# Pooled attention and SiLU MLP on one core: attention by token halves of the next tile instead of thirds of a batch, a ring of two tiles for x

## The chip, the core and the metric

The kernel runs on one core of a Trainium2 chip. TensorE (PE) does the matmuls, VectorE (DVE) and ScalarE (ACT) the elementwise work, GpSimd (POOL) pools keys and values in later tiles and issues most loads, SyncE (SP) issues the stores. The metric is the device time of one execution in microseconds (us), median of several runs. A span is the part of an execution that the profiler's instruction records cover.

## The reference

Eight batches of 576 tokens, eight heads of width 64. Keys and values are first averaged over groups of 8 positions, so that each head has 72 pooled keys. The attention output, 4608 tokens by 512 channels, is the input x of a two-layer network with 2048 hidden channels:

```python
k_p = k.reshape(B, H, Sp, pool, D).mean(axis=3)      # pool = 8, Sp = 72
v_p = v.reshape(B, H, Sp, pool, D).mean(axis=3)
scores = scale * np.matmul(q, k_p.transpose(0, 1, 3, 2))
scores = scores - np.max(scores, axis=-1, keepdims=True)
attn = np.exp(scores)
attn = attn / (np.sum(attn, axis=-1, keepdims=True) + 1e-09)
x = np.matmul(attn, v_p)      # heads side by side: 4608 x 512
h = x @ w_in                  # 512 x 2048
g = h * (1.0 / (1.0 + np.exp(-h)))
return g @ w_out              # 2048 x 512
```

## The kernel before

**Tiles and batches.** The network works on nine tiles of 512 tokens (`t` = 0 to 8), attention on eight batches of 576. The two don't line up: batch b ends 64 (b+1) tokens further on than tile b. While the matrix products of tile t run, the attention of batch t+1 is worked in between them; the last two tiles have none beside them. x (`xT`) lies in SBUF as a ring of 2304 columns (`NX = 4 * S`, four batches, 4.5 tiles).

**The matrix products.** Most of a tile is done by a Strassen-like scheme with seven products in place of eight 2x2 block products. In the first product there are four units of hidden channels (a, b, c, d), each with products 1 to 7 of two steps; in the second, products P1/Q1 to P7/Q7 (two halves of four steps). A step is two matmuls of 256 columns (one of 512 in the plain products `g`, `m`). `tile_products` walks an order written out by hand, such as `FOUR` (tiles 2 to 6) or `BARE` (7 and 8); `FIRST` and `THREE` are tiles 0 and 1, where weights and sums are still being loaded and made. Sums of blocks are made by DVE: `unit_x_sum` for x, `hidden_sum` for the hidden values, `weight_sum` and `unit_weight_sum` for weights. Each group of products goes through three PSUM banks A, E and B; `behind` copies A to B after product 1 (DVE), copies E to SBUF after product 5 (ACT, L738) and after product 6 adds B and that copy into E (DVE, L740). Product 7 then goes on adding into B, so it has to wait until L740 has read it.

**Attention work** is a list of fillers, `at(step, function)` or `late(step, function)`: `spread` runs each when the product's step has been issued. All engines get their instructions in program order; nothing is reordered. `third(n)` is a third of a batch: 192 positions of each of the two groups of four heads, 384 columns. `scores` does 16 matmuls of 192 columns into four banks (L414), then four exponentials on ACT (L425); `denominators` 4 matmuls of 384 columns (L435), then a logarithm and an exponential on ACT (L444, L445), which give the reciprocal; `numerators` 16 matmuls (L464) and two multiplications on DVE that write x (L476). In a middle tile they stand at steps 63 (scores of third 0), 77 (scores 1 and denominators 0), 87 (denominators 1, numerators 0 and the numerators of the batch before's third 2), 94 (scores 2), 103 (denominators 2) and 106, or 103 again (numerators). Tile 6 does its own third 2 as well. Batch 0 is done ahead of tile 0 in halves of 256 positions (`scores0` and so on), and its last 64 positions ride along in tile 0 (`rest`).

**PSUM** has eight banks: a pool of three (`mm`) for the products' B banks and the second product, one of five (`at`) for attention and the units' A and E.

**ACT tables.** The exponentials and logarithms need another function table than SiLU. `attn_tables` (L483) and `moe_tables` (L486) load one, 1.28 us each; the latter stands ahead of every tile.

**Loads.** Up to tile 1 everything comes through POOL's queue, in the order of the program: the rest of batch 0's queries, keys of batch 1, `w_out` quarter 0, all queries of batch 1, `w_out` 1 to 3, values of batch 1, then, as fillers, the keys of batch 2 in two halves, the second of which is added onto the first by the transfer itself (`load_half_2`), with the queries of batch 2 between them, and the values of batch 2 in the same way. Each load waits for the landing of the one eight before it in the program (they share eight semaphores in turn). The second halves' sums over the pooled positions are made by DVE in `slot_sums` (L260), for batch 2 at step 2 of tile 1.

Of the kernel before, what the change touches and what calls it, by code (L numbers as in the profile page):

```python
# [36 lines left out]
def kernel(  # L37
# [21 lines left out]
    HS = S // 2  # L59

    KQ, NQ, CQ = KG // 2, NTT // 2, d_model // 2

    NX = 4 * S
# [4 lines left out]
    QF = QI // 2  # L68
    DH = D // 2
    VW = max(HS, 2 * S // 3)  # L70
# [44 lines left out]
    xT = singles.tile([128, KF, NX], BF16, name="xT")  # L115
# [17 lines left out]
    def load_q(b, halves=False):  # L133
        st = batches.setdefault(b, {})
        q_bf = mid.tile([128, 2, QI * D], BF16, tag="q_bf", name="q_bf")
        if halves:
            pass
        elif b == B - 1:

            for s in range(4):  # L140
                for a in range(2):
                    nc.gpsimd.dma_start(
                        out=q_bf[QP * s : QP * (s + 1), a, :].rearrange(
                            "p (i d) -> p i d", d=D
                        ),
                        in_=q[b, 4 * a + s].rearrange("(i p) d -> p i d", p=QP),
                    )
        else:
            nc.gpsimd.dma_start(out=q_bf, in_=q_r[b])
        st["q_bf"] = q_bf  # L150
        st["qT"] = mid.tile([128, 2, QI, QP, 2], BF16, tag="qT", bufs=1, name="qT")


    def q_transpose(b, a, f):
        q_positions(b, a, f * QF, (f + 1) * QF, batches[b]["qT"][:, a, f * QF : (f + 1) * QF])

    def q_positions(b, a, i0, i1, dst):
        nc.vector.transpose(
            out=dst.rearrange("r i p c -> r (i p c)").bitcast(FP32),
            in_=batches[b]["q_bf"][:, a, i0 * D : i1 * D].bitcast(FP32),  # L160
        )
# [143 lines left out]
    def copy_v(b, a, copy=nc.vector.tensor_copy, heads=4):  # L305
# [5 lines left out]


    IP = NQ // QP
    QR = QI - 2 * IP
    flat = [x.rearrange("p a b -> p (a b)") for x in h_sum]
    es_wide = flat[0][:SP].rearrange("k (s n) -> k s n", s=4)
    rec0 = flat[1].bitcast(FP32).rearrange("r (f g n) -> r f g n", f=2, g=2)
    wide32 = flat[2].bitcast(FP32)
    lnd_wide, rec_wide = wide32[:, :512], wide32[:, 512:]
    qT_rest = flat[3][:, : 2 * QR * 2 * QP].rearrange(  # L320
        "r (a i p c) -> r a i p c", a=2, i=QR, p=QP
    )

    def q_transpose0(a, f):
        cols = slice(f * IP, (f + 1) * IP)
        q_positions(0, a, f * IP, (f + 1) * IP, batches[0]["qT"][:, a, cols])

    def q_transpose_rest(a):
        q_positions(0, a, 2 * IP, QI, qT_rest[:, a])

    def scores0(pool, g, f):
        st = batches[0]
        sc = [pool.tile([128, 2, 512], FP32, tag="sc2", bufs=2, name="sc_ps") for _ in range(2)]
        for c in range(2):
            for s in range(4):
                rows = slice(32 * s, 32 * (s + 1))
                nc.tensor.matmul(
                    sc[s // 2][:SP, s % 2, :NQ],
                    lhsT=kz[0][rows, g, c, :],
                    rhs=st["qT"][rows, g, f * IP : (f + 1) * IP, :, c],  # L340
                    start=(c == 0), stop=(c == 1),
                )
        es = mid.tile([SP, 4, VW], BF16, tag="es", bufs=4, name="es")[:, :, :NQ]
        for j in range(2):
            nc.scalar.activation(
                es[:, 2 * j : 2 * j + 2, :], sc[j][:SP, :, :NQ], func=AF.Exp,
                scale=score_scale,
            )
        st["es", g, f] = es

    def denominators0(den_ps, f):
        for g in range(2):
            for s in range(4):
                nc.tensor.matmul(
                    den_ps[32 * s : 32 * (s + 1), g * NQ : (g + 1) * NQ],
                    lhsT=ones, rhs=batches[0]["es", g, f][:, s, :], start=True, stop=True,
                )
        nc.scalar.activation(lnd_wide, den_ps, func=AF.Ln)

    def reciprocals0(f):  # L360
        nc.scalar.activation(
            rec0[:, f].rearrange("r g n -> r (g n)"), lnd_wide, func=AF.Exp, scale=-1.0
        )

    def numerators0(nu_ps, g, f):
        st = batches[0]
        es = st.pop(("es", g, f))
        nu = nu_ps.rearrange("r (c n) -> r c n", c=2)
        for c in range(2):
            for s in range(4):  # L370
                nc.tensor.matmul(
                    nu[32 * s : 32 * (s + 1), c, :],
                    lhsT=st["vp"][:, 4 * g + s, c::2], rhs=es[:, s, :],
                    start=True, stop=True,
                )
        return nu

    def x_of(nu, g, f):
        nc.vector.tensor_mul(
            out=xT[:, 2 * g : 2 * g + 2, f * NQ : (f + 1) * NQ], in0=nu,  # L380
            in1=rec0[:, f, g : g + 1, :].broadcast_to([128, 2, NQ]),
        )

    QV = QI // 3

    def third(n):
        return tuple((g, n * QV, (n + 1) * QV) for g in range(2))

    def width(segs):
        return QP * sum(i1 - i0 for _, i0, i1 in segs)  # L390

    def seg_cols(segs):
        o = 0
        for g, i0, i1 in segs:
            n = QP * (i1 - i0)
            yield g, i0, i1, slice(o, o + n)
            o += n

    def rest_cols(segs, g):
        o, n = width(segs), QR * QP  # L400
        return slice(o + g * n, o + (g + 1) * n)

    def scores(b, segs, rest=False):
        st = batches[b]
        w = width(segs) + 2 * QR * QP * rest
        sc = [ps_tile([128, 512], FP32, "at", "sc_ps")[:SP, :w] for s in range(4)]
        jobs = [(g, b, st["qT"][:, g, i0:i1], cs) for g, i0, i1, cs in seg_cols(segs)]
        if rest:
            jobs += [(g, 0, qT_rest[:, g], rest_cols(segs, g)) for g in range(2)]
        for g, bk, qT, cs in jobs:  # L410
            for c in range(2):
                for s in range(4):
                    rows = slice(32 * s, 32 * (s + 1))
                    nc.tensor.matmul(  # L414
                        sc[s][:, cs],
                        lhsT=kz[bk % 2][rows, g, c, :],
                        rhs=qT[rows, :, :, c],
                        start=(c == 0), stop=(c == 1),
                    )
        if rest:  # L420
            es = es_wide
        else:
            es = mid.tile([SP, 4, VW], BF16, tag="es", bufs=4, name="es")[:, :, :w]
        for s in range(4):
            nc.scalar.activation(es[:, s, :], sc[s], func=AF.Exp, scale=score_scale)  # L425
        st["es", segs] = es


    def denominators(b, segs):
        st = batches[b]  # L430
        es = st["es", segs]
        w = es.shape[-1]
        den_ps = ps_tile([128, 512], FP32, "at", "den_ps")
        for s in range(4):
            nc.tensor.matmul(  # L435
                den_ps[32 * s : 32 * (s + 1), :w],
                lhsT=ones, rhs=es[:, s, :], start=True, stop=True,
            )
        if w > VW:
            lnd, rec = lnd_wide, rec_wide  # L440
        else:
            rec = mid.tile([128, VW], FP32, tag="rec", bufs=4, name="rec")[:, :w]
            lnd = mid.tile([128, VW], FP32, tag="lnd", name="lnd")[:, :w]
        nc.scalar.activation(lnd, den_ps[:, :w], func=AF.Ln)  # L444
        nc.scalar.activation(rec, lnd, func=AF.Exp, scale=-1.0)  # L445
        st["rec", segs] = rec

    def numerators(b, segs, rest=False):
        st = batches[b]
        w = width(segs)  # L450
        g0, i0, i1 = segs[0]
        c0 = b * S % NX + i0 * QP
        cols = slice(c0, c0 + (i1 - i0) * QP)
        es = st.pop(("es", segs))
        rec = st.pop(("rec", segs))
        jobs = [(g, st["vp"], cs) for g, _, _, cs in seg_cols(segs)]
        if rest:
            jobs += [(g, batches[0]["vp"], rest_cols(segs, g)) for g in range(2)]
        nu = []
        for c in range(2):  # L460
            nu_ps = ps_tile([128, 512], FP32, "at", "nu_ps")
            for g, vp, cs in jobs:
                for s in range(4):
                    nc.tensor.matmul(  # L464
                        nu_ps[32 * s : 32 * (s + 1), cs],
                        lhsT=vp[:, 4 * g + s, c::2],
                        rhs=es[:, s, cs],
                        start=True, stop=True,
                    )
            nu.append(nu_ps)  # L470
        ng = len(segs)
        done = [(c, slice(0, w), cols) for c in range(2)]
        if rest:
            done += [(c, slice(w, w + 2 * QR * QP), slice(2 * NQ, S)) for c in range(2)]
        for c, ws, xs in done:
            nc.vector.tensor_mul(  # L476
                out=xT[:, 2 * g0 + c : 2 * (g0 + ng - 1) + c + 1 : 2, xs],
# [630 lines left out]
```

## Time and profile before

| | us |
|---|---|
| median of 3 runs | 278.34 (278.17 to 278.71) |
| the profiled execution | 278.52 |
| its span | 276.7 |
| granted TensorE clock | 1.0 of full speed throughout |
| DVE, ACT busy | 208.5, 191.6 |

Where the tiles lie in the span, by the first matmul of each (timeline of PE):

| tile | from | to | length | attention worked in it |
|---|---|---|---|---|
| 0 | 17.8 | 51.48 | | batch 1 and 64 positions of batch 0 |
| 1 | 51.48 | 81.12 | 29.64 | batch 2 |
| 2 to 5 | 81.12 | 194.70 | 28.36, 28.43, 28.42, 28.37 | batches 3 to 6 |
| 6 | 194.70 | 223.61 | 28.91 | batch 7 |
| 7 | 223.61 | 248.21 | 24.60 | none |
| 8 | 248.21 | 276.7 | 28.5 with the last stores | none |

A page of the profile has, for each group of equal instructions, the busy time, the mean duration of one, and the idle time of its engine just ahead of them with the engine that ended it. A timeline row is: start, length, engine, line, operation, output and inputs, shapes, count, and in brackets idle time of that engine ahead of it and what ended it. Matmuls overlap: the time that one takes away is read from start to start (0.109 us for 256 columns, 0.218 for 512), not from its length.

### The profile page before, as it was taken

The numbers are of one execution on the slowest core, as the hardware profiler recorded it, in microseconds if no ns is written. First come the engines' busy times: TensorE is split into PE (matmuls) and PEld (weight loads), VectorE is DVE, ScalarE is ACT, GpSimd is POOL, SyncE is SP. The second block draws the span as 40 slices with busy tenths as digits, with TensorE's granted clock in tenths as the row PEclk, the third lists the DMA queues.
The fourth block names the chain that finished last, engine by engine and source line by source line (L and its number), as shares of the span: only waits on it lengthen the run. The fifth ranks groups of instructions, "written<-read, shape, count | busy, mean of one in ns | idle before, by whom it ended". The sixth has DMA issues, their size and how long they took to land.

```text
span 276.7 us, 7362 instructions
## 1 busy us (share of the span) xinstructions
PE 269.3 (97%) x3000; PEld 212.5 (77%) x3000; DVE 208.5 (75%) x381; ACT 191.6 (69%) x365; POOL 98.4 (36%) x104
## 2 busy tenths in 40 slices
PE   8999899999999999999999999999999999999994
PEld 4368544488788878887888778877887788888883
DVE  4868857987998777877787787768787786766872
ACT  1578758578769785979498958985798578409710
POOL 8657314262138620962088219850900000000000
PEclk9999999999999999999999999999999999999999
DMA  7999999967738797559655965999410042005004
GB/s 214 270 204 288 208 292 222 238 123 165 142 73 158 218 161 133 142 152 170 102 140 152 167 107 121 219 109 139 124 31 2 1 105 51 0 12 130 16 0 152
DMA packets 31761, 37.72 MB, mean 136 GB/s; under 512 B 10640, under 2 KB 22672, under 8 KB 31728
## 3 DMA queue, kind: packets, MB, share of 16 engines
q0 software_dynamic: 24080, 26.64, 52.3%
q1 hardware_dynamic: 7216, 9.97, 13.0%
q10 hardware_dynamic: 432, 0.66, 0.6%
q8 instruction: 23, 0.38, 0.6%
q14 instruction: 10, 0.08, 0.2%
HBM read 36.70 MB, written 9.44 MB: 167 GB/s over the span
## 4 chain that ended last, share of the span: by engine, by line
PE 87%; DVE 4%; issue 1%; ACT 1%; DVEq 0%
PE o_psB L725 16%; PE u_psB L706 15%; PE o_psA L725 10%; PE u_psE L706 10%; PE o_psE L725 10%; PE u_psA L706 10%; PE o_ps L623 4%; PE sc_ps L414 4%; PE nu_ps L464 2%; PE den_ps L435 2%; PE hp_ps L564 1%; DVE w_sum L538 1%; DVE xT L476 1%; ACT h_T L744 1%; DVE u_psE L740 1%
## 5 line engine op out<-in xcount | busy, mean ns | idle before, releaser
L706 PEld LDWEIGHTS <-w_sum 128*128 128x128 bf16 x528 | 51.3, 98 | 7.2 <-issue 1.2
L725 PEld LDWEIGHTS <-h_sum 128*128 128x128 bf16 x512 | 48.4, 98 | 8.8 <-issue 1.2
L706 PEld LDWEIGHTS <-w_in_sb 128*128 128x128 bf16 x396 | 38.7, 98 | 4.9
L725 PEld LDWEIGHTS <-h_T 128*128 128x128 bf16 x384 | 36.6, 98 | 6.1 <-issue 1.1
L706 PE MATMUL u_psB<-x_sum,w_sum 128*128 128x256 bf16 x264 | 39.1, 272 | 0.8 <-DVE u_psE L740 0.8
L706 PE MATMUL u_psA<-xT,w_in_sb 128*128 128x256 bf16 x264 | 39.8, 273 | 0.0
L425 ACT ACTIVATE es<-sc_ps 72x384 bf16<-72x384 f32 x80 | 32.2, 481 | 9.7 <-PE sc_ps L414 9.7
L725 PE MATMUL o_psB<-w_sum,h_sum 128*128 128x256 bf16 x256 | 32.7, 273 | 0.3 <-DVE o_psE L740 0.3
L725 PE MATMUL o_psA<-w_out_sb,h_T 128*128 128x256 bf16 x256 | 31.9, 272 | 0.0
L740 DVE TENSOR_TENSOR u_psE<-u_psB,p 128x512 f32<-128x512 f32 x33 | 22.4, 696 | 10.2 <-ACT p L738 8.6
L735 DVE COPY u_psB<-u_psA 128x512 f32<-128x512 f32 x31 | 21.4, 698 | 9.8 <-PE u_psA L706 9.8
L744 ACT ACTIVATE h_T<-u_psE 128x512 bf16<-128x512 f32 x33 | 19.7, 597 | 12.4 <-PE u_psE L706 12.4
L757 DVE TENSOR_TENSOR c<-u_psB,p 128x512 f32<-128x512 f32 x33 | 22.5, 682 | 4.3 <-PE u_psB L706 3.5
L188 POOL TENSOR_TENSOR raw<-raw 72x1024 f32<-72x1024 f32 x10 | 23.6, 2361 | 0.0
L744 ACT ACTIVATE h_T<-u_psB 128x512 bf16<-128x512 f32 x33 | 19.8, 600 | 4.4 <-PE u_psB L706 4.4
L649 DVE TENSOR_TENSOR h_sum<-h_T 128x1024 bf16<-128x1024 bf16 (+1 forms) x31 | 21.3, 699 | 1.1 <-ACT h_T L744 1.1
L744 ACT ACTIVATE h_T<-u_psA 128x512 bf16<-128x512 f32 x33 | 20.1, 608 | 1.5 <-PE u_psA L706 1.3
L744 ACT ACTIVATE h_T<-c 128x512 bf16<-128x512 f32 x33 | 21.0, 637 | 0.0
L649 DVE TENSOR_TENSOR h_sum<-h_T,h_sum 128x1024 bf16<-128x1024 bf16 (+1 forms) x24 | 20.4, 855 | 0.1
L706 PE MATMUL u_psE<-x_sum,w_sum 128*128 128x256 bf16 x132 | 19.8, 273 | 0.0
L706 PE MATMUL u_psE<-x_sum,w_in_sb 128*128 128x256 bf16 x132 | 19.8, 273 | 0.0
L476 DVE TENSOR_TENSOR xT<-nu_ps,rec 128x384 bf16<-128x384 f32 x40 | 19.7, 548 | 0.0
(108 smaller groups left out, 452.4 us busy)
## 6 DMA issues: line engine op xcount, KB each, us to landing
out_dram<-o_sb SPq DMA_DIRECT2D x128, 64.0 KB, 1.7
raw<-in_k_dram POOLq DMA_DIRECT2D x10, 576.0 KB, 8.5
raw<-in_v_dram POOLq DMA_DIRECT2D x10, 576.0 KB, 8.2
q_bf<-in_q_dram POOLq DMA_DIRECT2D x6, 576.0 KB, 9.7
w_in_sb<-in_moe_w_in_dram POOLq DMA_DIRECT2D x8, 256.0 KB, 8.0
w_out_sb<-in_moe_w_out_dram POOLq DMA_DIRECT2D x4, 512.0 KB, 12.2
raw<-in_v_dram POOLq DMA_DIRECT2D x2, 768.0 KB, 11.8
raw<-in_k_dram POOLq DMA_DIRECT2D x1, 768.0 KB, 8.8
```

What stands on the lines that cost most here:

```text
L188: nc.gpsimd.tensor_add(out=raw[:, :, : 2 * D], in0=raw[:, :, : 2 * D], in1=raw[:, :, 2 * D :])
L414: nc.tensor.matmul(sc[s][:, cs], lhsT=kz[bk % 2][rows, g, c, :], rhs=qT[rows, :, :, c], start=(c == 0), stop=(c == 1),)
L425: nc.scalar.activation(es[:, s, :], sc[s], func=AF.Exp, scale=score_scale)
L476: nc.vector.tensor_mul(out=xT[:, 2 * g0 + c : 2 * (g0 + ng - 1) + c + 1 : 2, xs], in0=nu[c][:, ws].rearrange("r (g n) -> r g n", g=ng), in ...
L623: nc.tensor.matmul(ps["m", m], lhsT=h_T[:, g, m * 128 : (m + 1) * 128], rhs=w_out_sb[:, g, :], start=(g == 0), stop=(g == KG - 1),)
L649: nc.vector.tensor_tensor(out=h_sum[n][:, k0:k1, :], in0=get(a), in1=get(b), op=op)
L706: nc.tensor.matmul(ps[y, BANK[n]][:, u, :], lhsT=w[:, kk, 128 * u : 128 * (u + 1)], rhs=x[:, kk, :], start=n in (1, 5) and u == 0 and kk == 0,
L725: nc.tensor.matmul(o_bank(n, c), lhsT=left(n, kt, c), rhs=w[:, kt, :], start=n in (1, 5) and kt == 0 and c == 0, stop=kt == KQ - 1, skip_g ...
L735: (acopy if t == 0 else vcopy)(ps[y, "B"], ps[y, "A"])
L740: tt(out=ps[y, "E"], in0=ps[y, "B"], in1=f32[y], op=add)
L744: nc.scalar.activation(h_T[:, g : g + 2, j * NQ : (j + 1) * NQ], src, func=AF.Silu)
L757: tt(out=c22, in0=ps[y, "B"], in1=f32[y], op=add)
```

## The change

Attention is cut by the tiles of the network. In tile t, for t = 0 to 7, the 512 positions of tile t+1 are worked as two halves of 256. A half that lies over the end of a batch takes two sets of matmuls (`half_units`), one for each batch, into the same banks. Scores, denominators and products of a half fill their banks (512 columns). x is a ring of two tiles; the transposed queries (`qT`) hold one tile. The fillers stand at three places of a middle tile: 63 (scores of half 0), 79 (scores of half 1, denominators of half 0) and 93 (denominators of half 1, all numerators); x is written by `x_half` at 93 and 97, the x sums stand at 105 in every tile, and the SiLU table is loaded at 94. Tile 7 uses `FOUR` and has the attention of tile 8 beside it.

In `FOUR` and `THREE` the second half of product 2 moves from two places to between Q6 and P7. In `FIRST`, two steps of the plain product m0 move ahead of d7, the others ahead of d4, and m3 (now in an `at` bank) goes ahead of the last quarter of the others. The queries of batch 1 are loaded in two pieces of 14 and 4 positions (of 18), for two head groups each: four transfers in place of one. The values of batch 1 go ahead of `w_out` 3, and the second piece behind it. The queries of later batches are loaded at step 33.

```diff
-    NX = 4 * S
+    UH = NQ // QP
+    UT = NTT // QP
...
-    xT = singles.tile([128, KF, NX], BF16, name="xT")
+    xT = singles.tile([128, KF, 2 * NTT], BF16, name="xT")
+    qT = singles.tile([128, 2, UT, QP, 2], BF16, name="qT")
...
+    def half_units(t, f):
+        for b, i0, i1, u in q_units(t, UH * f, UH * (f + 1)):
+            o = QP * (u - UH * f)
+            yield b, slice(u, u + i1 - i0), slice(o, o + QP * (i1 - i0))
+
+    def scores(t, f):
+        sc = [ps_tile([128, 512], FP32, "at", "sc_ps")[:SP] for s in range(4)]
+        for g in range(2):
+            score_matmuls(sc, t, f, g, g * NQ)
+        es = half_state(t, f)["es"] = es_tile()
         for s in range(4):
             nc.scalar.activation(es[:, s, :], sc[s], func=AF.Exp, scale=score_scale)
...
+    def x_half(t, f):
+        st = half_state(t, f)
         for c in range(2):
             nc.vector.tensor_mul(
+                out=xT[:, c::2, x_cols(t, f)],
+                in0=st["nu"][c].rearrange("r (g n) -> r g n", g=2),
+                in1=st["rec"].rearrange("r (g n) -> r g n", g=2),
             )
...
-    load_q(1)
-    for c in range(1, 4):
+    load_q(1, halves=True)
+    load_q_part(1, 0, 2 * UT - QI)
+    for c in range(1, 3):
         load_w_out(c)
     for i0, i1 in ((0, 3), (3, 4), (4, 5)):
         load_slots(nc.gpsimd, 1, "v", i0, i1)
+    load_w_out(3)
+    load_q_part(1, 2 * UT - QI, QI)
...
-    HEAD = "P1 ds Q1 d4 P2 o2:4-5 P5 Q5 P6 Q6 o2:5-8 P7 Q7 P3 Q3 P4 Q4"
+    HEAD = "P1 ds Q1 d4 P2 P5 Q5 P6 Q6 Q2 P7 Q7 P3 Q3 P4 Q4"
...
     FIRST = (
-        "p4.0 p6.0 p0.1 p2.1 c1 p4.1 c5 p6.1 c6 c2 c7 d1 c3 d5 c4 d6 cs d2 d7 m0:0-4 d3 ds d4"
-        " m1:0-4 m2:0-4 m0:4-8 m1:4-8 m2:4-8 m0:8-12 m1:8-12 m2:8-12"
-        " m0:12-16 m1:12-16 m2:12-16 m3:0-16"
+        "p4.0 p6.0 p0.1 p2.1 c1 p4.1 c5 p6.1 c6 c2 c7 d1 c3 d5 c4 d6 cs d2 m0:0-2 d7 d3 m0:2-4 ds d4"
+        " m1:0-4 m2:0-4 m0:4-8 m1:4-8 m2:4-8 m0:8-12 m1:8-12 m2:8-12 m3:0-12"
+        " m0:12-16 m1:12-16 m2:12-16 m3:12-16"
     )
...
             late(63, attn_tables)
-            for n, (sc, den) in enumerate(zip((63, 77, 94), (77, 87, 103))):
-                late(den, denominators, a, visits[n])
-                late(sc, scores, a, visits[n])
-            nu_at = (87, 103, 106)
-            for n, sg in enumerate(visits):
-                if n < 2 or t >= B - 2:
-                    late(nu_at[n], numerators, a, sg)
-                if n == 0 and 1 < t < B - 1:
-                    late(nu_at[n], numerators, a - 1, visits[2])
+            late(63, scores, a, 0)
+            late(79, scores, a, 1)
+            late(79, denominators, a, 0)
+            late(79, reciprocals, a, 0)
+            late(93, denominators, a, 1)
+            late(93, reciprocals, a, 1)
+            for n in range(2):
+                late(93, numerators, a, n)
+            late(93, x_half, a, 0)
+            late(94, moe_tables)
+            late(97, x_half, a, 1)
         if t < NT - 1:
             for n in (0, 2, 1, 3):
-                late(105 if t < 4 else 96 if t < B - 1 else 84, unit_x_sum, t + 1, n)
-        moe_tables()
+                late(105, unit_x_sum, t + 1, n)
```

## The prediction

> **What bounds the kernel now.** I read the busy shares first, then the stages.
>
> ```profile
> PE 269.3 (97%) x3000; PEld 212.5 (77%) x3000; DVE 208.5 (75%) x381; ACT 191.6 (69%) x365; POOL 98.4 (36%) x104
> ...
> 109.50:137.90 28.40, 28.40 (x338) 23.84 (x336) 21.80 (x39) 22.23 (x43) 12.75 (x10) 1.00 0.71 141
> ...
> 223.60:248.20 24.60, 24.60 (x226) 21.81 (x225) 18.01 (x29) 13.05 (x23) 0.00 (x0) 1.00 0.17 41
> ```
>
> The lower rows are busy times by stage (length, PE, weight loads, DVE, ACT, POOL, clock, DMA share, GB/s) of tile 3 and tile 7. PE is busy throughout and its list of waits sums to only some 3 us, so the time is what PE has to issue. A tile's 112 steps take 112 x 0.2186 = 24.48 us; tile 7, without attention, takes 24.60. Attention costs tile 3 some 3.9 us. The timeline of PE in tile 2 shows on what:
>
> ```profile
> 94.78 0.60 PE L706 MATMUL u_psB<-xT,w_sum 128*128 128x256 bf16 x4
> 95.31 0.54 PE L414 MATMUL sc_ps<-qT,kz 32*72 32x192 bf16 x16
> 95.80 1.25 PE L725 MATMUL o_psA<-w_out_sb,h_T 128*128 128x256 bf16 x10
> ...
> 98.64 0.38 PE L725 MATMUL o_psB<-w_sum,h_sum 128*128 128x256 bf16 x2
> 98.95 0.37 PE L435 MATMUL den_ps<-es,ones 72*32 72x384 bf16 x4
> 99.25 0.54 PE L414 MATMUL sc_ps<-qT,kz 32*72 32x192 bf16 x16
> 99.72 1.70 PE L725 MATMUL o_psB<-w_sum,h_sum 128*128 128x256 bf16 x14
> 101.26 0.82 PE L725 MATMUL o_psA<-w_out_sb,h_T 128*128 128x256 bf16 x6
> 102.01 0.35 PE L435 MATMUL den_ps<-es,ones 72*32 72x384 bf16 x4
> 102.18 0.83 PE L464 MATMUL nu_ps<-es,vp 72*32 72x192 bf16 x32
> 102.95 1.70 PE L725 MATMUL o_psB<-w_sum,h_sum 128*128 128x256 bf16 x14
> ```
>
> Take the products' starts, at 0.109 us a matmul, out of each gap. The first interruption costs 95.80 - (94.78 + 0.44) = 0.58; denominators and scores 99.72 - 98.86 = 0.86; denominators and two numerators 102.95 - 101.91 = 1.04. Two more in the tile cost 0.57 and 0.70. Sum 3.75; with the keys' transpose 0.13 and 24.48 this is 28.36, tile 2's length. Four matmuls run side by side: sixteen of 192 columns stream for 4 x 192 x 0.000427 = 0.33 us (0.000427 us a column from 0.109 per 256), so of the first 0.58 some 0.25 is change-over, before (0.09) and after.
>
> **Attention in halves, tiles 2 to 7.** The columns in all stay the same; the interruptions fall from five to three. Widening 192 to 256 adds 4 x 64 x 0.000427 = 0.11 to each sixteen, and 384 to 512 adds 0.05 to denominators. So: scores 0.69; scores and denominators 0.86 + 0.11 + 0.05 = 1.02; denominators and four sets of sixteen (two before) 1.04 + 0.05 + 2 x 0.11 = 1.31. Sum 3.02 against 3.75. A half over a batch's end splits its matmuls: in tile 0 now, 192 and 64 columns together take 0.60 where 256 would take 0.47 + 0.11, so 0.03 for each kind, 0.06 for a tile (1, 2, 4, 5 and 6).
>
> The new order puts back a wait. After product 6, L740 must read B before product 7 goes on:
>
> ```profile
> 28.46 0.60 PE L706 MATMUL u_psB<-x_sum,w_sum 128*128 128x256 bf16 x4
> 28.90 0.60 PE L706 MATMUL u_psA<-xT,w_in_sb 128*128 128x256 bf16 x4
> 29.92 0.60 PE L706 MATMUL u_psB<-x_sum,w_sum 128*128 128x256 bf16 x4 [0.42 <-DVE u_psE L740]
> ```
>
> Issue of product 6 ends at 28.90, product 7 starts at 29.92: 1.02. (c6 and c7 at 24.82 and 26.28, and product 6 and 7 of tile 1 at 73.57 and 74.59, give 1.02 too.) Between Q6 and P7 stand now six matmuls, denominators and numerators; afterwards only Q2's eight, 0.87. PE waits 0.15 in each of tiles 1 to 7. Bounds: 0, if L740 is quicker, and 0.4, as at 29.92; the three equal rows decide.
>
> A middle tile is then 24.48 + 0.13 + 3.02 + 0.15 and 0.05 on the mean = 27.83. Tiles 2 to 5: 113.58 now, 4 x 27.83 = 111.3 after, -2.3. Tile 6 (28.91 now, with its own third 2 at 0.54): -1.1. Tile 7 gets attention, without a keys' transpose: 24.48 + 3.02 + 0.15 = 27.65, +3.05. Together -0.3: what the cuts save, the eighth attended tile and the new wait take back.
>
> **What lies beside PE there.** Sixty-four exponentials of 512 columns in place of 80 of 384 and four of 512 (0.59 and 0.48 us), and a table pair of 2 x 1.28 more in tile 7: ACT has 13.05 of 24.60 us there, so they are hidden. x of the next tile is now finished in the last microseconds. Count from the end of Q6 = T. Product 7 starts at T+1.02; denominators and numerators go in after step 93, at T+2.33 to 3.63; Q3 ends at T+5.82, the tile at T+7.57. DVE: first x half T+3.2 to 4.4 (multiplication 0.6 from start to start, as L740), the sum behind Q7 to 5.0, second x half to 6.2 (its reciprocal is ready at T+5: 0.5 and 0.6 on ACT after T+3), E's copy from 6.1 to 6.8, four x sums (108.88 to 110.55 now, 1.67) to 8.45, then unit a's copy to 9.15. Next tile: a5 needs the first sum, ready at 7.2, at 8.04; a6 needs the copy at 9.35, 0.2 later than it is there. Nothing waits, but 0.2 is all the cover; each 0.1 beyond it costs 0.1 in seven tiles.
>
> **Tile 0.** Products m0:0-2 fill the wait at 29.92 (gain 0.44), and the wait of 0.39 to 0.55 ahead of the first m2 matmul (33.51) goes, since ACT gets d3 0.85 earlier: together 1.0. `w_out` 0 has landed at 29.45 (issued 20.95, 8.5 to landing), 0.1 after m0:0-2 wants it. The first scores then come at 35.0 but wait for the transposed queries: DVE starts these at 34.28 as now, two of 448 columns at some 0.6 (0.47 for 288, 0.43 for 256, a nanosecond a column), done at 35.45; 0.45 of the gain goes. Interruptions: now 0.69, 0.89, 0.84, 0.37, 0.66, 0.55, 0.54 = 4.54; after 0.69, 1.02, 0.37, 1.10 = 3.18. So tile 0 would end near 49.3 instead of 51.48.
>
> But tile 1 can't use it:
>
> ```profile
> 54.84 0.42 DVE L260 TENSOR_TENSOR raw<-raw 128x256 f32<-128x256 f32 x1 [0.37 <-DMA raw<-in_k_dram]
> 55.29 0.29 DVE L260 TENSOR_TENSOR k<-raw 128x128 bf16<-128x128 f32 x1
> 55.88 0.70 DVE L735 COPY u_psB<-u_psA 128x512 f32<-128x512 f32 x1 [0.30 <-PE u_psA L706]
> ```
>
> DVE sits at 54.84 until the last piece of batch 2's keys has landed, and the copy that b6 needs is next in its queue; after the change nothing in that queue moves in between. DMA share is 0.9 to 1.2 from 15 to 55, so what counts is the bytes ahead, and these are the same: values and `w_out` 3 change places, two small query pieces go behind them. The three extra transfers push those that wait for the eighth before them: the first halves of batch 2's keys go out at about 34.5, 37 and 39.4 (landings of `w_out` 1 at 34.8, `w_out` 2 at 37.3, values 42.3 less their move forward) instead of 31.8, 33.2 and 35.1, still ahead of the 44 at which the transfers before them end. So I leave 54.84. The copy runs 55.55 to 56.25, b6 starts at 56.3 (56.92 now), where PE would have come at 54.8 to 55.5. Of 2.2 gained, 0.6 is left. Bounds: 0, if the keys come 0.6 later, and 2.1, if they come before 53.3. `w_out` 3 itself moves from a landing at 39.9 to about 43.3; m0:12 wants it at 44.1.
>
> The Trainium skill speaks against the split of the query load: DMA: Bandwidth & Descriptors, Measured (HBM→SBUF, 128 partitions, SWDGE, issued from GpSimd), advises to batch towards 1 MiB, and Anatomy of one DMA there puts some 2.0 us of fixed cost on each. If the three extra ones paid that one after another, the keys would come 6 us later by the page's figure and the whole would end near 283 by this estimate. No row before shows such a serial cost.
>
> The row for it: landings of `w_out` 0, the queries (576 KB) and `w_out` 1, at 29.45, 32.2 and 34.8, while issue to landing is 8.5 to 11.3; transfers in the full queue cost their bytes, not their latency. I take nothing for the split, and up to 1 us (half of the spread from 8.5 to 10.7 of queries and `w_out` 0) for the range.
>
> **Tile 1 after b6.** Now 3.74 of attention (0.59, 0.86, 1.02 with 0.31 of waiting for L740, 0.57, 0.70); after 3.08 + 0.15: -0.5. **Tile 8** is unchanged, a wait of 0.03 apart.
>
> **Sum:** -0.6 (to b6), -0.5 (rest of tile 1), -0.3 (tiles 2 to 7), -0.03 = -1.45. The profiled execution is 278.52 (span 276.7 and 1.82 around it), 0.18 above the median; 278.52 - 1.45 = 277.1, or 276.9 beside the median 278.34.
>
> **Rivals.** First, the gain of tile 0 comes through: the second halves of the keys are issued when the first land (45.35 now), and the store of m0 at 43.6 is out of their way afterwards. Against it, the DMA share near 1 up to 55. Then -1.45 - 1.5 = -2.95: 275.4.
>
> Second, on the other side: the chain of DVE at the tile's end is late. Place: a6 of tiles 2 to 8; price: seven times what the chain exceeds its 0.2 of cover. For it: DVE has 9.15 - 3.2 = 6 us with hardly a gap, and a6 already starts 0.06 late in tile 3 (110.79 to 111.29, 0.50 instead of 0.44). Against it: that chain today has two multiplications more behind the copy of E. Slower than before from 0.2 + 1.45/7 = 0.41 late; at 0.6, +2.8 - 1.45 = +1.35: 279.7.
>
> Third, the change-overs are not saved, since they go with the kinds of matmuls rather than with the places: then tiles 1 to 6 gain half of 0.73 and tile 7 costs 0.35 more, so +2.2 + 0.35 goes onto -1.45: +1.1, 279.4. Against it: the denominators at 102.01 go straight on to the numerators in 0.17, their streaming time.
>
> Fourth, no difference: the waits at L740 are 0.3, so -1.45 + 7 x 0.15 = -0.4: 277.9.
>
> **How the numbers follow.** Forecast 0.48, first rival 0.20, second 0.12, third 0.06, fourth 0.14. What a measurement can tell from no change is about 0.2%, 0.56 us. Faster: 0.48 + 0.20, and 0.02 for a fourth rival at half its price = 0.70; within 0.2%: 0.13; slower: 0.17. Range: down to the first rival, 275.3; up, with 1 us for the keys and 0.4 of the waits, to 278.4. The forecast's own range, without rivals, is 276.2 to 277.8.
>
> **What will show it.** Middle tiles of 27.7 to 27.9 us and tile 7 of 27.6; three interruptions of 0.7, 1.0 and 1.3; a wait of 0.15 ahead of each P7, ended by DVE L670 (the old L740); in tile 1 a wait of 0.8 to 1.5 ahead of b6, ended by DVE, which waited for keys near 54.8. Wrong it is if the tiles' first steps show waits for x or its sums, if the keys land before 53.5 or after 56, or if m0's last quarter waits for `w_out`.

## The result, and the profile after

| | before | after |
|---|---|---|
| median, us | 278.34 (278.06 to 279.54, 13 runs) | 276.17 (275.44 to 277.67, 13 runs) |
| profiled execution, span, us | 278.52, 276.7 | 276.11, 274.3 |

The ratio is 0.9925, with an interval of 0.9907 to 0.9942: faster by 2.2 us. Forecast were 276.9, in a range of 275.3 to 278.4. The direction and the middle tiles came as written; two terms did not, by -1.76 and +0.96 us, and they pulled in opposite directions. So it is partly luck that the total came within 0.7 of the forecast.

The time by stages, first matmul to first matmul, from the timeline of PE:

| stage | before | forecast of the difference | after | difference |
|---|---|---|---|---|
| to b6 of tile 1 | 56.92 | -0.6 | 54.56 | -2.36 |
| the rest of tile 1 | 24.20 | -0.5 | 23.78 | -0.42 |
| tile 2 | 28.36 | -0.5 | 28.82 | +0.46 |
| tiles 3 to 5 | 85.22 | -1.7 | 83.27 | -1.95 |
| tile 6 | 28.91 | -1.1 | 27.77 | -1.14 |
| tile 7 | 24.60 | +3.05 | 27.62 | +3.02 |
| tile 8 | 28.49 | 0 | 28.49 | 0 |

The busy line of the page after, and the same windows as before the change (length, PE, weight loads, DVE, ACT, POOL, clock, DMA share, GB/s) for tile 3 and tile 7:

```profile
PE 267.4 (97%) x2967; PEld 213.6 (78%) x2972; DVE 209.6 (76%) x368; ACT 191.3 (70%) x337; POOL 99.9 (36%) x107
```

```profile
107.16:134.90 27.74, 27.74 (x303) 23.48 (x300) 21.43 (x37) 21.06 (x37) 12.66 (x10) 1.00 0.83 165
218.19:245.81 27.62, 27.62 (x299) 23.35 (x297) 21.30 (x35) 20.83 (x36) 0.00 (x0) 1.00 0.16 39
```

PE is still busy from end to end. Tile 7 now looks like tile 3: it has attention, and nearly the same length. The timeline of PE in tile 3 shows the three places:

```profile
120.83 0.60 PE L636 MATMUL u_psB<-xT,w_sum 128*128 128x256 bf16 x4
121.36 0.65 PE L331 MATMUL sc_ps<-qT,kz 32*72 32x256 bf16 x16
121.94 1.05 PE L655 MATMUL o_psA<-w_out_sb,h_T 128*128 128x256 bf16 x8
...
124.57 1.04 PE L655 MATMUL o_psB<-w_sum,h_sum 128*128 128x256 bf16 x8
125.53 0.65 PE L331 MATMUL sc_ps<-qT,kz 32*72 32x256 bf16 x16
126.11 0.40 PE L363 MATMUL den_ps<-es,ones 72*32 72x512 bf16 x4
126.45 1.05 PE L655 MATMUL o_psB<-w_sum,h_sum 128*128 128x256 bf16 x8
127.33 1.04 PE L655 MATMUL o_psA<-w_out_sb,h_T 128*128 128x256 bf16 x8
128.35 1.47 PE L655 MATMUL o_psB<-w_sum,h_sum 128*128 128x256 bf16 x12
129.75 0.40 PE L363 MATMUL den_ps<-es,ones 72*32 72x512 bf16 x4
129.98 1.05 PE L378 MATMUL nu_ps<-es,vp 72*32 72x256 bf16 x32
130.96 0.61 PE L655 MATMUL o_psB<-w_sum,h_sum 128*128 128x256 bf16 x4
```

Take out the products at 0.1092 us each, as before: 121.94 - (120.83 + 0.44) = 0.67; 126.45 - (124.57 + 0.87) = 1.01; 130.96 - (128.35 + 1.31) = 1.30. The sum is 2.98. Between Q2 at 127.33 and P7 at 128.35 lie 1.02 us, 0.15 more than Q2's eight matmuls take: the wait that the new order was to bring.

What was not foreseen stands at two places. The first is the keys of batch 2, in the timeline of DVE around the start of tile 1:

```profile
52.72 0.42 DVE L261 TENSOR_TENSOR raw<-raw 128x256 f32<-128x256 f32 x1 [0.36 <-DMA raw<-in_k_dram]
```

This is the row that stood at 54.84 before: the last piece landed 2.1 us earlier. Tile 1 began at 49.36, and b6 followed at 54.56, right behind c5: it waited for nothing.

The second is tile 2. The timelines of POOL, DVE and PE there:

```profile
88.50 2.36 POOL L189 TENSOR_TENSOR raw<-raw 72x1024 f32<-72x1024 f32 x1 [2.21 <-DMA raw<-in_v_dram]
90.94 1.59 POOL L192 TENSOR_TENSOR vp<-raw 72x512 bf16<-72x512 f32 x1
```

```profile
88.77 0.68 DVE L687 TENSOR_TENSOR c<-u_psB,p 128x512 f32<-128x512 f32 x1
89.37 2.03 DVE L579 TENSOR_TENSOR h_sum<-h_T 128x1024 bf16<-128x1024 bf16 x1
```

```profile
92.45 0.60 PE L636 MATMUL u_psB<-xT,w_sum 128*128 128x256 bf16 x4 [0.29 <-DVE c L687]
92.98 0.84 PE L331 MATMUL sc_ps<-qT,kz 32*72 32x192 bf16 x32
94.15 1.03 PE L655 MATMUL o_psA<-w_out_sb,h_T 128*128 128x256 bf16 x8 [0.33 <-DVE o_psB L665]
```

POOL waited 2.21 us for the values of batch 3. Its pooling then ran while DVE was to make a hidden sum, and that sum took 2.03 us where the others take 0.68. The DVE instructions behind it came late, and PE waited for two of them. Before the change the pooling was over at 91.53, and the first hidden sum began at 92.15 (POOL and DVE of the kernel before):

```profile
87.80 2.38 POOL L188 TENSOR_TENSOR raw<-raw 72x1024 f32<-72x1024 f32 x1
90.26 1.27 POOL L191 TENSOR_TENSOR vp<-raw 72x512 bf16<-72x512 f32 x1
```

```profile
92.15 0.68 DVE L649 TENSOR_TENSOR h_sum<-h_T 128x1024 bf16<-128x1024 bf16 x1
```

Tile 2 now begins 2.8 us earlier, but the values come 1.1 us later: their second half landed at 88.42, before the change at 87.34. The first half was asked for 3.5 us earlier (68.26 for 71.75) and took 10.8 us to land, where it had taken 6.8.

### The profile page after: what moved, and what is told of

Same layout as the page of the kernel before. It is cut to its first block, busy times and chain, and to the rows that moved or that the text cites. A ratio compares the mean times of both kernels' runs of the same rounds, so it can differ in the third digit from the quotient of the medians.

```text
span 274.3 us, 7266 instructions
## 1 busy us (share of the span) xinstructions
PE 267.4 (97%) x2967; PEld 213.6 (78%) x2972; DVE 209.6 (76%) x368; ACT 191.3 (70%) x337; POOL 99.9 (36%) x107
## 4 chain that ended last, share of the span: by engine, by line
PE 86%; DVE 5%; issue 1%; ACT 0%; DVEq 0%; ACTq 0%
PE o_psB L655 16%; PE u_psB L636 15%; PE o_psE L655 10%; PE u_psE L636 10%; PE o_psA L655 10%; PE u_psA L636 10%; PE o_ps L553 5%; PE sc_ps L331 3%; PE nu_ps L378 3%; PE den_ps L363 2%; PE hp_ps L496 1%; DVE w_sum L474 1%; DVE h_sum L579 1%; DVE u_psE L670 1%; DVE xT L396 0%
## 5 line engine op out<-in xcount | busy, mean ns | idle before, releaser
L356 ACT ACTIVATE es<-sc_ps 72x512 bf16<-72x512 f32 x64 | 32.7, 590 | 5.9 <-PE sc_ps L331 5.8
L670 DVE TENSOR_TENSOR u_psE<-u_psB,p 128x512 f32<-128x512 f32 x33 | 23.0, 698 | 9.2 <-ACT p L668 5.4
L413 DVE TENSOR_TENSOR xT<-nu_ps,rec 128x512 bf16<-128x512 f32 x32 | 20.5, 684 | 11.2 <-PE nu_ps L378 11.2
L189 POOL TENSOR_TENSOR raw<-raw 72x1024 f32<-72x1024 f32 x10 | 24.2, 2415 | 2.3 <-DMA raw<-in_v_dram 2.2
L579 DVE TENSOR_TENSOR h_sum<-h_T 128x1024 bf16<-128x1024 bf16 x32 | 23.1, 726 | 0.2 <-ACT h_T L674 0.2
L668 ACT COPY p<-u_psE 128x512 f32<-128x512 f32 x33 | 19.6, 593 | 4.6 <-PE u_psE L636 4.6
L636 PE MATMUL u_psB<-xT,w_sum 128*128 128x256 bf16 x132 | 19.6, 272 | 0.3 <-DVE c L687 0.3
```

Of the source, the lines that this page charges most:

```text
L189: nc.gpsimd.tensor_add(out=raw[:, :, : 2 * D], in0=raw[:, :, : 2 * D], in1=raw[:, :, 2 * D :])
L413: nc.vector.tensor_mul(out=xT[:, c::2, x_cols(t, f)], in0=st["nu"][c].rearrange("r (g n) -> r g n", g=2), in1=st["rec"].rearrange("r (g n) ...
L579: nc.vector.tensor_tensor(out=h_sum[n][:, k0:k1, :], in0=get(a), in1=get(b), op=op)
L636: nc.tensor.matmul(ps[y, BANK[n]][:, u, :], lhsT=w[:, kk, 128 * u : 128 * (u + 1)], rhs=x[:, kk, :], start=n in (1, 5) and u == 0 and kk == 0,
L668: acopy(f32[y], ps[y, "E"])
L670: tt(out=ps[y, "E"], in0=ps[y, "B"], in1=f32[y], op=add)
```

## The experiments

All are edits of the changed kernel (276.17, ratio to before 0.9925) unless another base is named. Each was run beside the kernel before, whose medians were 278.35 to 278.56. Executions with the same code ahead of tile 1 enter tile 1 at 48.7 to 49.6, so a start of a tile is compared to some 0.5 us and the length of a tile to 0.03.

### The load order for tile 2

```diff
-                at(16, load_rest, 3, "k")
                 at(33, load_q, 3)
+                at(34, load_rest, 3, "k")
```

> The changed kernel with one difference in tile 1: the queries of batch 3 are issued before the second half of the keys of batch 3, not behind it. Seen after the change: the values of batch 3 landed late (POOL waited 2.21 us for them in tile 2), POOL's pooling of them then ran beside a hidden sum of DVE, which took 2.03 us instead of 0.68, and TensorE waited 0.29 and 0.33 us in tile 2 (28.8 us long, the other middle tiles 27.75). Theory one, a late transfer: pooling ends before the first hidden sum, that sum takes 0.7 us, tile 2 takes 27.8 us, the whole about 1.0 us less than the changed kernel (some 3.2 us less than before). Theory two, DVE's queue in tile 2 is too full whatever POOL does (two transposes of 320 columns ahead of the bank copy): tile 2 stays at 28.8 and the total at the changed kernel's.

Measured 276.37 (ratio 0.9918, 0.9897 to 0.9939): no difference, and tile 2 took 28.86. The queries' place alone was not it: the values' first half, asked for at 68.08, still took 9.7 us, the second half 11.3, POOL waited 4.97 us for it and pooled at 89.97, and a hidden sum of 2.07 us lay beside it. Since the landing did not come forward, this run does not yet decide between the two theories.

### The prologue's loads, and the end of tile 0

Loads as before:

```diff
-    load_q(1, halves=True)
-    load_q_part(1, 0, 2 * UT - QI)
-    for c in range(1, 3):
+    load_q(1)
+    for c in range(1, 4):
         load_w_out(c)
...
-    load_w_out(3)
-    load_q_part(1, 2 * UT - QI, QI)
```

> The changed kernel with the loads ahead of tile 0 as they were: queries of batch 1 in one transfer, the quarter 3 of the output weights ahead of the values. Question: why the last piece of the keys of batch 2 landed at 52.7 us and not at 54.8. Theory one, the stores of tile 0 (they come later after the change, out of the way of the keys): the keys still land near 52.7 (52.3 to 53.5). Theory two, order and split of the loads: they land near 54.8. In both the values of batch 1 come some 3 us later, DVE has their sums at 45.6 instead of 42.4, and the values' selection in tile 0 waits some 1 to 1.5 us; the total is then 1 to 1.5 us above the changed kernel, less what the wait in tile 2 changes.

Measured 277.15 (0.9951, 0.9934 to 0.9967). The keys' last piece came at 53.99. In tile 0 PE waited 0.5 for the values' sums; in tile 2 it waited 0.8 and 0.3, beside a hidden sum of 2.54. So the loads give 0.7 (by the ratios, whose intervals just overlap) to 1.0 us (by the medians) of the 2.2.

The end of `FIRST` as before, with m0's store earlier:

```diff
-        " m1:0-4 m2:0-4 m0:4-8 m1:4-8 m2:4-8 m0:8-12 m1:8-12 m2:8-12 m3:0-12"
-        " m0:12-16 m1:12-16 m2:12-16 m3:12-16"
+        " m1:0-4 m2:0-4 m0:4-8 m1:4-8 m2:4-8 m0:8-12 m1:8-12 m2:8-12"
+        " m0:12-16 m1:12-16 m2:12-16 m3:0-16"
```

> The changed kernel with the end of tile 0's order as it was (m0, m1 and m2 finished before m3), so that their stores go out some 2 to 3 us earlier, as before the change; loads stay in the new order. Theory one (stores): the keys of batch 2 land later than 52.7, near 54 to 54.8, and the product b6 of tile 1 waits for DVE. Theory two (loads): they land near 52.7. In both m0's last quarter comes at 41.4, before the quarter 3 of the output weights lands (42.4), and waits about 1 us; total 0.5 to 2 us above the changed kernel.

Measured 276.52 (0.9926, 0.9899 to 0.9953), the same, where 0.5 to 2 us more was expected. PE waited 1.3 for the last quarter of `w_out`, so tile 1 began later, at 50.13. But the keys were there by 52.68, though the stores were issued at 43.87, as before the change. Tile 2 was 27.85 long: it began at 79.11, and the hidden sum beside the pooling took only 1.06.

Both parts as before:

> Both the prologue's loads and the end of tile 0's order as before; attention by halves stays. With each alone the keys of batch 2 had landed at 53.99 (loads as before) and no later than 52.68 (end of tile 0 as before). Theory one (the order of the loads alone moves the keys; the earlier store of m0 doesn't matter): keys at 54.0 plus or minus 0.2, total near 277.3 (the two single losses, 0.98 and 0.35, added). Theory two (m0's store matters once the loads are late): keys back at 54.8, total near 278.

Measured 277.24 (0.9960, 0.9937 to 0.9983), the keys at 54.11. With these four the store is out: early or late, the keys come at 52.7 with the new loads and at 54.0 to 54.1 with the old ones. What remains to 54.84 of before, 0.7, none of these edits explains; it is less than this row moves between kernels with the same code up to there (52.48 to 53.77).

The two parts of the new loads, each alone. First, values ahead of `w_out` 3, the queries in one transfer:

```diff
-    load_q(1, halves=True)
-    load_q_part(1, 0, 2 * UT - QI)
+    load_q(1)
...
     load_w_out(3)
-    load_q_part(1, 2 * UT - QI, QI)
```

> Of the change's prologue loads only one part is kept: the values of batch 1 go ahead of the last quarter of w_out. The queries of batch 1 come in one transfer again. Theory one (what brings the keys of batch 2 forward is the values' place: they land at 39 to 40 instead of 42.3, so that a place in the turn of eight transfers comes free earlier): keys' last piece at 52.7 as after the change, against 54.0 with all loads as before; no wait of 0.5 for the sums of values in tile 0; total near 276.2. Theory two (it is the split of the queries): keys at 54.0, total near 276.8.

Then the split alone:

```diff
-    for c in range(1, 3):
+    for c in range(1, 4):
         load_w_out(c)
...
-    load_w_out(3)
     load_q_part(1, 2 * UT - QI, QI)
```

> The other part alone: the queries of batch 1 in two pieces for two head groups each, the second piece last; the values stay behind all of w_out. Theory one (the values' place decides): values landed after 42, a wait of some 0.5 of PE for their sums near 45 in tile 0, keys' last piece at 54.0, total near 277.2. Theory two (the split decides): keys at 52.7, only the 0.5 of tile 0 lost, total near 276.7. A serial fixed cost for each transfer, three more of them, would bring the keys to 56 or later and the total over 278.

Values ahead: 276.10 (0.9927, 0.9899 to 0.9955), as the whole change. Split alone: 276.92 (0.9944, 0.9927 to 0.9960), and 0.9 of waiting for the values' sums in tile 0. The sums of the keys' last piece, in the timeline of DVE, first with the values ahead and then with the split:

```profile
52.15 0.42 DVE L261 TENSOR_TENSOR raw<-raw 128x256 f32<-128x256 f32 x1
```

```profile
53.98 0.43 DVE L261 TENSOR_TENSOR raw<-raw 128x256 f32<-128x256 f32 x1 [0.42 <-DMA raw<-in_k_dram]
```

In the first row DVE no longer waits for the transfer at all. The values' place moves the keys; three transfers more neither cost nor gain. The fixed cost that the Trainium skill names (DMA: Bandwidth & Descriptors, Anatomy of one DMA) does not show one after another in this queue.

### The wait ahead of P7

Scores of half 1 and denominators of half 0 four steps later, so that they stand between Q6 and Q2:

```diff
-            late(79, scores, a, 1)
-            late(79, denominators, a, 0)
-            late(79, reciprocals, a, 0)
+            late(83, scores, a, 1)
+            late(83, denominators, a, 0)
+            late(83, reciprocals, a, 0)
```

> The changed kernel with the second interruption (scores of half 1, denominators of half 0) moved from step 79 to step 83, between product 6 and product 7, where TensorE waits 0.15 us in each of tiles 1 to 7. Theory: the interruption takes the place of the wait, each tile is 0.15 us shorter (middle tiles 27.6), the total about 1.0 us less than the changed kernel. Rival: the exponentials of half 1 come 0.9 us later on ACT, the denominators at step 93 wait for them by as much as is saved, and the total stays.

Measured 274.99 (0.9871, 0.9852 to 0.9891). The timeline of PE in tile 3 of this kernel:

```profile
125.67 0.65 PE L331 MATMUL sc_ps<-qT,kz 32*72 32x256 bf16 x16
126.25 0.40 PE L363 MATMUL den_ps<-es,ones 72*32 72x512 bf16 x4
126.58 1.05 PE L655 MATMUL o_psA<-w_out_sb,h_T 128*128 128x256 bf16 x8
127.47 1.47 PE L655 MATMUL o_psB<-w_sum,h_sum 128*128 128x256 bf16 x12
```

P7 now follows Q2 after 0.89 us, 0.02 more than its matmuls take. Tiles 3 to 6 are 27.60 to 27.63 long, tile 7 27.46: 0.14 to 0.16 less in each.

### Five places again, with the halves

```diff
-            late(79, denominators, a, 0)
-            late(79, reciprocals, a, 0)
+            late(89, denominators, a, 0)
+            late(89, reciprocals, a, 0)
             late(93, denominators, a, 1)
             late(93, reciprocals, a, 1)
-            for n in range(2):
-                late(93, numerators, a, n)
+            late(93, numerators, a, 0)
...
+            late(96, numerators, a, 1)
```

> Five interruptions per middle tile again, with the columns and matmuls of the halves unchanged: denominators of half 0 go alone to step 89, the numerators of half 1 alone to step 96. Theory (a change-over costs about 0.25 us at each place where attention goes in between products, whatever the number of columns): two places more in tiles 1 to 7 give middle tiles near 28.25 instead of 27.75, and 14 x 0.25 = +3.5 us in all, near 279.7. Rival one (the cost goes with the columns and kinds of matmuls, not with the places): tiles stay at 27.75, total near 276.2. Rival two (a smaller change-over of 0.1, the streaming before and after overlapping): +1.4, near 277.6. The wait ahead of P7 stays 0.15 either way, since only Q2 stands between Q6 and P7.

Measured 278.30 (0.9999, 0.9987 to 1.001), between rival two and the theory. Middle tiles take 28.07 to 28.11. PE in tile 3:

```profile
128.28 0.60 PE L655 MATMUL o_psB<-w_sum,h_sum 128*128 128x256 bf16 x4
128.81 0.40 PE L363 MATMUL den_ps<-es,ones 72*32 72x512 bf16 x4
129.14 1.05 PE L655 MATMUL o_psB<-w_sum,h_sum 128*128 128x256 bf16 x8
130.12 0.40 PE L363 MATMUL den_ps<-es,ones 72*32 72x512 bf16 x4
130.34 0.61 PE L378 MATMUL nu_ps<-es,vp 72*32 72x256 bf16 x16
130.88 0.61 PE L655 MATMUL o_psB<-w_sum,h_sum 128*128 128x256 bf16 x4
131.33 0.38 PE L655 MATMUL o_psE<-w_out_sb,h_sum 128*128 128x256 bf16 x2
131.64 0.62 PE L378 MATMUL nu_ps<-es,vp 72*32 72x256 bf16 x16
132.20 1.70 PE L655 MATMUL o_psE<-w_out_sb,h_sum 128*128 128x256 bf16 x14
```

Denominators alone cost 129.14 - (128.28 + 0.44) = 0.42, behind scores 1.01 - 0.67 = 0.34. Sixteen numerators alone cost 132.20 - (131.33 + 0.22) = 0.65; behind the other sixteen 1.30 - (130.88 - 130.01) = 0.43. So a place costs 0.08 with denominators and 0.22 with numerators. All five come to 3.29, against 3.75 before the change and 2.98 after it: of what a middle tile gains, 0.31 comes from fewer places. The other 0.46 is what remains, with six sets of matmuls for nine in five places; no run changes the sets alone.

### DVE and POOL side by side

Values pooled, and the next ones loaded, behind step 33 in tiles 2 to 6:

```diff
-                at(1, pool_v, a)
                 if a + 1 < B:
-                    at(1, load_one, a + 1, "v")
                     at(3, load_rest, a + 1, "k")
-                    at(4, load_rest, a + 1, "v")
                     at(33, load_q, a + 1)
+                at(40, pool_v, a)
+                if a + 1 < B:
+                    at(40, load_one, a + 1, "v")
+                    at(41, load_rest, a + 1, "v")
```

> GpSimd's pooling of the values moves in tiles 2 to 6 behind the loads of step 33, so that it runs about 11 to 16 us into the tile, beside the hidden sums of VectorE (steps 43 to 66), which are bf16 from SBUF to SBUF; nothing else changes. Theory (VectorE and GpSimd keep each other out there, as in tile 2 of the changed kernel, where a hidden sum took 2.03 instead of 0.68 us beside the pooling): in tiles 3 to 6 at least one hidden sum of over 1.2 us beside each pooling, PE waits of 0.2 to 0.7 in each of these tiles for VectorE, tiles near 28.2 instead of 27.75, total +1 to +3 us, 277.2 to 279. Rival (the late landing of the values alone made tile 2 long, by another way than VectorE, or the long hidden sum was a chance overlap with the transfers): hidden sums stay at 0.68, tiles 3 to 6 at 27.75, total near 276.2.

Measured 292.2 (1.048, 1.045 to 1.051), far past the expectation. Tiles 2 to 5 took 32.91, 32.24, 31.11 and 31.11; tile 6, where no loads stand ahead of the pooling and it begins 9.6 us into the tile, 28.01, with sums of 1.45 and 1.02. Tile 3 in the timelines of POOL, DVE and PE:

```profile
124.46 1.28 POOL L145 DMA_DIRECT2D q_bf<-in_q_dram  x1
125.21 2.91 POOL L189 TENSOR_TENSOR raw<-raw 72x1024 f32<-72x1024 f32 x1
128.19 1.60 POOL L192 TENSOR_TENSOR vp<-raw 72x512 bf16<-72x512 f32 x1
```

```profile
124.45 4.22 DVE L579 TENSOR_TENSOR h_sum<-h_T 128x1024 bf16<-128x1024 bf16 x1
128.60 0.43 DVE L159 STREAM_TRANSPOSE qT<-q_bf 128x256 f32<-128x256 f32 x1
128.96 0.66 DVE L665 COPY o_psB<-o_psA 128x512 f32<-128x512 f32 x1
129.53 0.81 DVE L579 TENSOR_TENSOR h_sum<-h_T 128x1024 bf16<-128x1024 bf16 x1
```

```profile
129.67 1.86 PE L655 MATMUL o_psA<-w_out_sb,h_T 128*128 128x256 bf16 x8 [2.94 <-DVE o_psB L665]
```

The first hidden sum ends at 128.67, 0.55 after POOL's addition (125.21 + 2.91 = 128.12); the second at 130.34, 0.55 after POOL's next one (128.19 + 1.60 = 129.79). In tile 2 of the changed kernel the same difference is 91.40 - 90.86 = 0.54; in the eight other kernels here with such a sum in tile 2 it took 1.06 to 2.70 us and ended 0.55 to 0.56 after POOL's addition. So the sum gets through when POOL's instruction is over; it does not run slowly beside it. The copy from PSUM and the transpose between them take their usual time while POOL works. The Trainium skill says it so (SBUF — State Buffer, Who interferes with whom): the port pair that both engines share is an exclusive lock, and a VectorE instruction with both inputs in SBUF contends with a GpSimd instruction that reads SBUF. These rows agree.

Tile 5 is long for another reason. There the eight loads of batch 7's queries stand ahead of the pooling, which begins only at 196.45; the hidden sums take 0.67 to 0.69. TensorE waits 1.52 us for the pooled values instead, and the sixteen matmuls of a product behind that wait take 3.29 us, where they take 1.75.

### The repair, and the best version

From the version with scores at 83: the values of batch 3 asked for right behind the first sums of batch 2's values, which move from step 69 to 56.

```diff
-                    at(69, slot_sums, "v", j, halves=True)
+                    at(56 if j == 0 else 69, slot_sums, "v", j, halves=True)
...
-                at(16, load_rest, 3, "k")
                 at(33, load_q, 3)
-                late(70, load_one, 3, "v")
+                at(57, load_one, 3, "v")
+                at(58, load_rest, 3, "k")
```

> From the best so far (scores of half 1 four steps later, 274.99): the first values of batch 3 are asked for in tile 1 some 5 us earlier, right behind the first sums of batch 2's values, ahead of the second half of batch 3's keys, and the queries of batch 3 ahead of both. Theory (tile 2 is long since its values land late, so that GpSimd's pooling falls beside VectorE's hidden sums): values of batch 3 land by 82, the pooling runs at about 85.5 to 89 and is over before the first hidden sum of two near 89.9, all hidden sums of tile 2 take 0.68 us, tile 2 is 27.6 to 27.7 long and the total about 0.4 to 1.0 us less, 274.0 to 274.6. Rival one (moving the first sums of values to step 56 delays VectorE in tile 1): PE waits of 0.3 or more near 62 in tile 1, which take back the gain. Rival two (the values land late whatever the order, as when the queries alone were moved): landing still at 88, no change.

Measured 273.68 (0.9846, 0.9811 to 0.9882). POOL and DVE in tile 2:

```profile
83.74 2.38 POOL L189 TENSOR_TENSOR raw<-raw 72x1024 f32<-72x1024 f32 x1
86.21 1.26 POOL L192 TENSOR_TENSOR vp<-raw 72x512 bf16<-72x512 f32 x1
```

```profile
88.80 0.68 DVE L579 TENSOR_TENSOR h_sum<-h_T 128x1024 bf16<-128x1024 bf16 x1
89.40 0.51 DVE L159 STREAM_TRANSPOSE qT<-q_bf 128x320 f32<-128x320 f32 x1
89.83 0.65 DVE L687 TENSOR_TENSOR c<-u_psB,p 128x512 f32<-128x512 f32 x1
90.40 0.67 DVE L579 TENSOR_TENSOR h_sum<-h_T 128x1024 bf16<-128x1024 bf16 x1
```

The pooling, with no wait ahead of it, is over at 87.47, 1.3 us before the first sum; both sums take their 0.68. Tile 2 is 27.63, as the others (28.84 with scores at 83 alone). No wait appeared near 62 in tile 1. By total time the intervals of this version and of scores at 83 alone overlap; the gain is read from tile 2. That DVE's queue is too full there whatever POOL does, the second theory of the first experiment, falls with it. This version beats both kernels.

## Why the prediction was right, and where it was wrong

**The middle tiles** were right by their parts: interruptions 0.67, 1.01 and 1.30 for 0.69, 1.02 and 1.31; a wait of 0.15 for 0.15; tiles of 27.74 to 27.77 for 27.83. The experiment at step 83 shows the wait alone: without it the kernel is 1.18 us faster, for 7 x 0.15 = 1.05 forecast. The reason given for the smaller interruptions, a change-over of 0.25 at each place, was too simple. That figure came from scores; two places less are worth 0.31 in a tile. The other 0.46, which goes with fewer and wider sets, the prediction's step by durations had counted in its sum without naming. The third rival (nothing saved with the places) falls, but more than half of the saving is not the places'.

**Tile 7** was right: +3.02 for +3.05. **Tile 6** was right: -1.14 for -1.1. **DVE's chain at the tile's end** held with its 0.2 of cover; the second rival's wait at a6 doesn't appear in the list of waits.

**Tile 0** ended at 49.36 for 49.3, but so close an agreement is luck. The gains as the prediction lists them, 1.0 + (4.54 - 3.18) - 0.45, add up to 1.9 and not to 2.2, which would end the tile at 49.6; and executions with the same code spread from 48.7 to 49.6.

**"But tile 1 can't use it"** was the step that failed. The prediction argued that the bytes ahead of the keys are the same, and wrote "So I leave 54.84". The keys landed at 52.6, before the 53.5 that it had named as a sign of being wrong, b6 waited for nothing, and the whole gain of tile 0 came through: -2.36 for -0.6. The size is that of the first rival; its reason is not. The experiments show no effect of m0's store, and that the place of the values ahead of `w_out` 3 brings the keys forward, with the same bytes in the queue. Since profiles with the same code differ here (the last piece at 52.4 to 53.7), it is best counted from the issue of `w_out` 0 over all kernels: 31.3 to 32.4 us in the eight with the values ahead, 33.2 to 33.8 in the four with the values behind, 1.5 us on the mean. By what way it does so stays open: 0.8 of it has been gained when the last piece is issued, since the first halves have landed earlier, and the last step from issue to landing is 0.7 shorter too.

**Tile 2** failed by a term that wasn't there: +0.46 for -0.5. The prediction costed the middle tiles as equal and followed the loads only up to the keys of batch 2. When a tile starts 2.8 us earlier, what is late next is the values of batch 3, which landed 1.1 later than before; DVE's sums then met POOL's pooling. The queries' new place at step 33 alone was not it (the first experiment). The values' own request stood behind the sums at step 69; moved forward, ahead of the second half of the keys and behind the queries, it takes the loss away. The two misses are not one: in the three kernels whose keys landed at 53.9 to 54.0, tile 2 began 0.8 to 1.2 us later than in the changed kernel, but the values of batch 3 came 1.4 to 1.7 later too, and the tile took 28.98 to 29.49 us.

## What to carry to other kernels

When a stage ends earlier, go through the transfers that the next stages wait for, one by one: a gain upstream can be taken back where a landing stays where it was. The cost of cutting work into pieces is read for each kind separately, alone and behind another kind (0.42 and 0.34, 0.65 and 0.43 here), not as one price for a place. And keep VectorE's sums from SBUF out of the time in which GpSimd computes: where they met in the worst place here, it cost 5.2, 4.5 and 3.4 us in tiles 2, 3 and 4, of which TensorE's lower clock (below) made 1.5 in tile 3.

## What the runs showed of the hardware that was not expected

**A sum also stood before POOL's addition began.** In the kernel with the late pooling the hidden sum stands from 124.45, 0.76 us before POOL's addition begins at 125.21; alone it would have been over by then. In tiles 2 and 4 it stands 0.92 and 0.95 us ahead of the addition (94.89 and 95.81, 156.62 and 157.57). Each time POOL was issuing two loads. The issue by itself does not hold a sum: in tile 5 four sums that began between 187.66 and 190.97 took 0.67 to 0.69 us while POOL issued loads from 187.13 to 193.19. What held the others stays open.

**PE's clock fell behind some of the waits.** The granted clock (the third number from the end) around the wait of 2.94 us in that kernel, by windows:

```profile
120.00:126.00 6.00, 6.00 (x57) 5.27 (x54) 5.16 (x8) 4.77 (x10) 2.39 (x3) 1.00 0.48 144
...
129.60:131.30 1.70, 1.63 (x8) 1.13 (x8) 1.70 (x4) 0.54 (x2) 1.05 (x2) 0.50 1.17 202
131.30:133.80 2.50, 2.50 (x19) 1.92 (x17) 2.08 (x3) 0.00 (x0) 0.00 (x0) 0.70 1.07 227
133.80:136.00 2.20, 2.20 (x33) 1.47 (x31) 0.00 (x0) 1.15 (x3) 0.00 (x0) 1.00 0.66 166
```

Eight matmuls then took 1.66 us from start to start where they take 0.87, sixteen 2.46 for 1.75: 1.5 us on top of the wait. The clock was 0.50 also behind the wait of 3.48 us in tile 2 (from 99.30 to 101.00), and behind the wait of only 1.52 us in tile 5 (from 201.30 to 203.00), but it stayed at 1.00 behind the wait of 3.01 us in tile 4. So the length of the wait alone does not tell. The Trainium skill speaks of a half clock after an idle window of about 3.4 us, and says that the window runs freely (TensorE: Matmul & The Clock Gate, Part 1). Tile 4 would fit that, since such a window can split a wait; the drops behind 2.94 and 1.52 us came with less idle time than the window, and no run here shows what counts as idle.
